# Turning the element-gradient tiles of a convolution stem through DRAM in one transfer, with reserves around transfers in the planned order

## The chip, the cores and the metric

The kernel runs on one core of one Trainium2 chip. The metric is device time in microseconds (us) of one execution. Three executions of the kernel before took 1305.70, 1307.24 and 1307.14 us; their median is 1307.14 us. A further execution was profiled, and its trace is what this document reads.

The engines are named as in the profile: PE (TensorE matmul), PEld (its weight load), DVE (VectorE), ACT (ScalarE), POOL (GpSimd) and SP (SyncE, which here only starts transfers). Transfers between DRAM and on-chip memory, and within on-chip memory, are DMAs; SP, ACT and POOL start them, each from its own queue and in program order.

## The reference

A strided convolution over time, a normalization over time for each batch and channel, and a GELU; and then all gradients of that for a given `grad_out`.

```python
B, T, D, K = 2, 16000, 256, 31          # x [2, 16000, 256], w [31, 256, 256], bf16
L = (T - K) // 2 + 1                    # 7985
h = sum(einsum('blc,cd->bld', x[:, i:i + 2 * L:2, :], w[i]) for i in range(K))
mu = h.sum(1)[:, None, :] / L
var = ((h - mu) ** 2).sum(1)[:, None, :] / L
h = (h - mu) / sqrt(var + 1e-5)
out = gelu(h * gn_gamma + gn_beta)      # tanh form
# returned: out, and the gradients of x, w, gn_gamma, gn_beta for grad_out
```

So there are three large products: the convolution itself, its transpose (the gradient of `x`, called the input gradient) and the correlation of `x` with the gradient at the convolution's output (the gradient of `w`).

## The kernel before

**Stages.** `forward` computes h for two batches b of four chunks c, from 0 to about 455 us. `input_grad` computes the gradient of x for the same eight chunks, from about 456 to 955 us. `weight_grad` ends the program. All three use a fast algorithm that adds and subtracts operands (on DVE) to need fewer products (on PE): each chunk goes through three branches A, B and C, and results in PSUM (four tiles `ps`) are moved, negated or combined by ACT (`keep`, L474; L917) and DVE (`ve`, `ve_neg`, L466 and L470) before PE can go on in the tile. A late ACT or DVE instruction there stops PE.

**The element-wise work in between.** `gelu_batch` and `gelu_unit` take h back from DRAM (`hd`, by a transfer from ACT's queue), take `grad_out` turned (a transposing transfer on SP, one for two units), compute out and the gradient before the normalization (ACT L714 to L738, DVE L718 to L740), store the latter (`dyd`, POOL) and turn out's tile for its store (a transposing transfer on SP). There are 16 units for each batch. Those of batch 0 run beside the forward pass of batch 1, and those of batch 1 beside the input gradient of batch 0.

`e_load` and `e_comp` make from `hd` and `dyd` the gradient at the convolution's output, for each chunk a tile `et` that has channels on partitions: two channel halves dh, two parities j and four phases k, with 256 positions each. It feeds PE at once. The weight gradient needs the same numbers with positions on partitions, and `dn_turn` makes them: 16 transposing transfers of 64 KB from `et` to the tile `DNO`, all on SP's queue, and then one POOL store of 1 MB to the DRAM tensor `dnd`. From `dnd`, `d2_piece` loads pieces (SP), takes differences (DVE, L1020) and stores them (`d2d`, POOL).

**What sets the order.** Every operation is first recorded by `Plan.add` with an engine, a duration and the tiles that it reads and writes. `Plan.order` then plays a schedule: each operation has a due time, worked out backwards from the position of the matmuls that need it (with `slack` for what no matmul needs soon; `PACE` gives the slack of the gelu units); at each step the engine that can start first takes its ready operation with the earliest due time. A transfer occupies its queue's engine for a while, then a shared server, and at most 8 may be under way for each of two groups. PE may take one of the next `look` matmul groups. The program is written in the order of the planned starts, and every engine then works through its own list in that order.

**Completion counters.** The built program has eight counters (DMAHW0 to DMAHW7) for the transfers that SP and ACT start, given out in turn, and eight more (DMASW0 to DMASW7) for POOL's. A transfer waits until the one that had its counter before has landed. Where such a wait stands in ACT's list, it holds all that follows on ACT.

Of the kernel before, what the change touches and what calls it, by code (L numbers as in the profile page):

```python
# [10 lines left out]
BF16 = mybir.dt.bfloat16  # L11
# [26 lines left out]
class Plan:  # L38
# [3 lines left out]
    def __init__(self, tc):  # L42
        self.tc = tc
        self.ops = []
        self.lastw = {}
        self.readers = {}
        self.pe = 0.0
        self.slack = 40.0
        self.hold = -1
        self.look = 6  # L50
        self.npe = 0

    def cells(self, ap):
# [48 lines left out]
    def order(self):  # L102
        ops = self.ops
# [5 lines left out]
        due = [0.0] * n  # L109
        for i in range(n - 1, -1, -1):  # L110
            o = ops[i]
# [8 lines left out]
        pes = [i for i, o in enumerate(ops) if o["eng"] == "PE"]  # L120
        rank = {i: k for k, i in enumerate(pes)}
        nextpe = 0
# [5 lines left out]
        free = {e: 0.0 for e in wait}  # L128
# [4 lines left out]
        while done < n:  # L133
# [27 lines left out]
                lane.append(end)  # L161
            ends[i] = end
            done += 1
            for s in succ[i]:
                r = end if ops[s]["eng"] == e and o["dma"] is None else end + 0.12
                if o["dma"] is not None and ops[s]["dma"] is not None:
                    r += 4.0
                ready[s] = max(ready[s], r)
                left[s] -= 1
                if not left[s]:  # L170
                    wait[ops[s]["eng"]].append(s)
# [15 lines left out]
def conv_stem_kernel(  # L187
# [28 lines left out]
    vl_d = [dram.tile([P, 3, 2, 2048], BF16, name=f"vl{i}") for i in range(3)]  # L216
    h_d = [[dram.tile([P, 4096], BF16, name=f"hd{b}_{c}") for c in range(NCK)] for b in range(NB)]
    dy_d = [[dram.tile([P, 4096], BF16, name=f"dyd{b}_{c}") for c in range(NCK)] for b in range(NB)]
    NDR = 192 + 8192 + 256
    dn_d = [dram.tile([NDR, D], BF16, name=f"dnd{b}") for b in range(NB)]  # L220
    d2_d = [dram.tile([9, P, 19 * D], BF16, name=f"d2d{b}") for b in range(NB)]
# [19 lines left out]
    def sb(off, *shape, dt=BF16):  # L241
        n = int(np.prod(shape)) * (2 if dt == FP32 else 1)
        assert off % 64 == 0 and off + 2 * n <= AR, (off, shape)
        v = arena[:, off // 2:off // 2 + n]
        if dt == FP32:
            v = v.bitcast(FP32)
        if len(shape) == 1:
            return v
        names = "abcdefg"[:len(shape)]
        return v.rearrange("p (" + " ".join(names) + ") -> p " + " ".join(names), **dict(zip(names, shape)))  # L250
# [5 lines left out]
    def load(out, in_, nbytes, run, eng="SP", slack=None, srcs=()):  # L256
        e = {"SP": nc.sync, "POOL": nc.gpsimd, "ACT": nc.scalar}[eng]
        add(eng, {"POOL": 0.8, "SP": 0.4, "ACT": 0.15}[eng], [out], [in_, *srcs], lambda: e.dma_start(out=out, in_=in_),  # L258
            dma=dcost(nbytes, run), slack=slack)

    def turn(out, in_, nbytes, slack=None):
        add("SP", 1.2 + max(0, nbytes - 262144) * 4.2e-6, [out], [in_],
            lambda: nc.sync.dma_start_transpose(out=out, in_=in_), dma=dcost(nbytes, 256), slack=slack)  # L263

    def zero(out, n, eng="POOL"):
# [565 lines left out]

    def dn_turn(b, c, o):
        et = ET[(4 * b + c) % 3]
        for dh in range(2):
            for j in range(2):
                for k in range(4):
                    turn(o[:, :, 4 * j + k, dh * P:(dh + 1) * P], et[:, dh, k, j, 0:HM], 65536)
        r0 = (192 if b else 0) + 2048 * c
        load(dn_d[b][r0:r0 + 2048, :].rearrange("(a p r) d -> p a (r d)", p=P, r=8),
             o.rearrange("p a r d -> p a (r d)"), 1 << 20, 4096, "POOL")  # L840

    def g_sums(t):
        et = ET[t % 3]
# [200 lines left out]
    DT = [sb(GREG, 15, D)]  # L1044
    D1T = sb(GREG + 7680, 2, 7, D)
    D2T = sb(GREG + 14848, 3, 2, 3, D)
    DNO = sb(GREG + 28928, 2, 8, D)


    xf = x.rearrange("b t c -> (b t) c")  # L1050
# [180 lines left out]

    RINGS = ((3, 2, 2, 2), (2, 1, 1, 2))
    D2AT = {(0, 0): (0, 1, 2), (0, 1): (3, 4), (1, 0): (5, 6)}
    PACE = ((15.0, 10.0), (40.0, 8.0))
    fw = forward()
    load_gb()
    add("DVE", 0.1, [JK], [], lambda: nc.vector.memset(JK, 0.0))
# [82 lines left out]
```

## Time and profile before

| | |
|---|---|
| median of three executions | 1307.14 us |
| profiled execution: its time, its span | 1306.86 us, 1305.1 us |
| PE busy, share of the span | 1235.0 us, 95% |
| DVE, ACT, POOL busy | 922.2, 492.5, 194.9 us |
| mean share of the 16 DMA engines, 450 to 850 us | 0.78 |
| transposing transfers on SP within on-chip memory | 160, of which 128 are those of `dn_turn` |

PE is busy nearly all the time, so time is to be found in the places where it stands still. A view that lists what each engine waited for, the timeline of one engine in a narrow window (idle time before an instruction stands in brackets with what ended it), and the chain of waits followed back from a late instruction show them. The view by windows gives the busy time of each engine in a stretch, then the clock that PE was granted (1.00 is full) and the mean busy share of the DMA engines.

### The profile page before, as it was taken

The page shows a single profiled execution, that of the slowest core. Times are in us where ns is not written, and L with a number is a line of the kernel's source. Part 1 is how long each engine was busy: PE and PEld are TensorE (multiplying, and loading weights), DVE is VectorE, ACT ScalarE, POOL GpSimd, SP SyncE. Part 2 cuts the span into 40 slices and gives each one's busy share as a digit, 9 for nine tenths or more (in the row PEclk, how much of TensorE's full clock was granted, in tenths as well). Part 3 has the DMA queues.
Part 4 walks back from the last instruction along what each step waited for, and adds up shares of the span by engine and source line. Part 5 has one row for each costly group of instructions (what it writes and reads, how often), then busy time and mean ns, then how long its engine had stood idle before and what let it go on. Part 6 is the DMA issues. An engine that isn't in the chain of part 4 may idle for free.

```text
span 1305.1 us, 19140 instructions
## 1 busy us (share of the span) xinstructions
PE 1235.0 (95%) x7746; PEld 759.7 (58%) x7746; DVE 922.2 (71%) x1164; ACT 492.5 (38%) x690; POOL 194.9 (15%) x293
## 2 busy tenths in 40 slices
PE   4999999999999989797899999899999999999998
PEld 2887799777778934343344444344466555556554
DVE  5978558789997678586786685557673885874462
ACT  0243243786863386566563223223221111112100
POOL 1002112111111011111120342123200000011021
PEclk9999999999999999898999999899999999999999
DMA  8644765959598869787784897768785698876610
GB/s 198 134 126 113 166 104 134 240 120 240 138 175 254 256 174 233 161 207 178 181 212 135 245 322 213 195 240 293 250 300 200 193 309 285 296 246 215 203 36 29
DMA packets 333177, 259.32 MB, mean 199 GB/s; under 512 B 195560, under 2 KB 311240, under 8 KB 326864
## 3 DMA queue, kind: packets, MB, share of 16 engines
q1 hardware_dynamic: 294448, 166.37, 51.4%
q0 software_dynamic: 21744, 83.34, 19.0%
q10 hardware_dynamic: 16896, 8.39, 2.6%
q8 instruction: 60, 0.98, 0.3%
q14 instruction: 29, 0.24, 0.1%
HBM read 128.32 MB, written 83.31 MB: 162 GB/s over the span
## 4 chain that ended last, share of the span: by engine, by line
PE 79%; DVE 7%; DMA 5%; SPq 3%; ACT 3%; issue 2%; POOL 0%; ACTq 0%; POOLq 0%; DVEq 0%
PE ps L391 32%; PE ps L1109 25%; PE ps L890 23%; SPq L263 2%; DVE arena L728 2%; DMA arena<-in_x_dram 1%; DMA arena<-in_grad_out_dram 1%; DMA arena<-dnd 1%; DMA arena<-arena 1%; DVE arena L849 1%; DVE ps L466 1%; DVE arena L718 1%; DMA d2d<-arena 1%; ACT arena L474 1%; DVE arena L1020 1%
## 5 line engine op out<-in xcount | busy, mean ns | idle before, releaser
L890 PE MATMUL ps<-arena 128*128 128x512 bf16 (+1 forms) x2112 | 459.9, 380 | 40.2 <-ACT ps L474 11.5
L391 PE MATMUL ps<-arena 128*128 128x256 bf16 (+3 forms) x3536 | 430.6, 283 | 19.4 <-DVE arena L349 17.7
L391 PEld LDWEIGHTS <-arena 128*128 128x128 bf16 x3536 | 345.9, 98 | 103.5 <-DVE arena L349 18.2
L890 PEld LDWEIGHTS <-arena 128*128 128x128 bf16 x2112 | 208.6, 99 | 291.0 <-issue 54.9
L1109 PE MATMUL ps<-arena 128*128 128x512 bf16 (+1 forms) x2016 | 343.8, 332 | 0.7 <-ACT ps L1202 0.7
L474 ACT ACTIVATE arena<-ps 128x1024 f32<-128x1024 f32 (+1 forms) x139 | 141.8, 1021 | 487.4 <-PE ps L890 219.6
L1109 PEld LDWEIGHTS <-arena 128*128 128x128 bf16 x2016 | 197.2, 98 | 144.1 <-issue 2.6
L359 DVE TENSOR_TENSOR arena<-arena 128x1088 bf16<-128x1088 bf16 (+3 forms) x182 | 155.4, 894 | 62.4 <-PE ps L391 54.5
L728 DVE TENSOR_TENSOR arena<-arena 128x1024 bf16<-128x1024 bf16 x160 | 109.6, 689 | 45.0 <-ACT arena L720 28.4
L258 POOL DMA_DIRECT2D out_dram<-arena x81 | 58.6, 726 | 457.3 <-DVE arena L1141 321.3
L1072 DVE TENSOR_TENSOR arena<-arena 128x4096 bf16<-128x4096 bf16 x42 | 95.4, 2287 | 34.3 <-DMA arena<-in_x_dram 25.6
L466 DVE TENSOR_TENSOR ps<-ps,arena 128x1024 f32<-128x1024 f32 x68 | 82.2, 1225 | 29.8 <-PE ps L1109 21.9
L849 DVE TENSOR_TENSOR arena<-arena 128x514 bf16<-128x514 bf16 (+3 forms) x152 | 71.4, 520 | 29.9 <-PE ps L890 28.7
L1020 DVE TENSOR_TENSOR arena<-arena 128x768 bf16<-128x768 bf16 (+3 forms) x112 | 63.7, 635 | 18.8 <-DMA arena<-dnd 18.3
L494 ACT ACTIVATE arena<-ps 128x512 bf16<-128x512 f32 (+1 forms) x64 | 37.1, 581 | 100.8 <-PE ps L391 99.4
L1190 DVE TENSOR_TENSOR arena<-arena 128x2304 bf16<-128x2304 bf16 x36 | 48.2, 1352 | 33.7 <-PE ps L1109 33.7
L258 POOL DMA_DIRECT2D d2d<-arena x70 | 50.8, 726 | 107.5 <-DVE arena L1020 100.2
L258 POOL DMA_DIRECT2D dyd<-arena x32 | 24.2, 758 | 229.3 <-DVE arena L728 208.6
L258 POOL DMA_DIRECT2D vl<-arena x36 | 26.1, 725 | 167.7 <-DVE arena L349 89.1
L474 ACT ACTIVATE ps<-ps 128x1024 f32<-128x1024 f32 x31 | 31.2, 1008 | 44.4 <-PE ps L1109 18.5
L718 DVE SCALAR_TENSOR_TENSOR arena<-arena 128x1024 bf16<-128x1024 bf16 x32 | 39.0, 1218 | 10.2 <-ACT arena L716 10.2
L349 DVE TENSOR_TENSOR arena<-arena 128x1024 bf16<-128x1024 bf16 (+2 forms) x37 | 36.8, 1016 | 7.6 <-DMA arena<-in_w_dram 5.2
(80 smaller groups left out, 638.7 us busy)
## 6 DMA issues: line engine op xcount, KB each, us to landing
arena<-in_x_dram SPq DMA_DIRECT2D x52, 1024.0 KB, 7.5
arena<-d2d SPq DMA_DIRECT2D x16, 1216.0 KB, 9.3
out_dram<-arena POOLq DMA_DIRECT2D x14, 1024.0 KB, 5.5
d2d<-arena POOLq DMA_DIRECT2D x30, 384.0 KB, 7.2
arena<-dnd SPq DMA_DIRECT2D x10, 960.0 KB, 7.0
vl<-arena POOLq DMA_DIRECT2D x36, 256.0 KB, 4.6
arena<-vl SPq DMA_DIRECT2D x9, 1024.0 KB, 5.8
hd<-arena POOLq DMA_DIRECT2D x8, 1024.0 KB, 6.0
```

Source lines behind the costliest of these rows:

```text
L258: add(eng, {"POOL": 0.8, "SP": 0.4, "ACT": 0.15}[eng], [out], [in_, *srcs], lambda: e.dma_start(out=out, in_=in_), dma=dcost(nbytes, run), ...
L359: lambda: nc.vector.tensor_tensor(out=o, in0=a, in1=b, op=ALU.add))
L391: yield nc.tensor.matmul(ps[:, dh, cs], lhsT=wt, rhs=mv, start=s0, stop=False, skip_group_check=True)
L466: add("DVE", dve(1024, 1), [out], [a, b], lambda: nc.vector.tensor_tensor(out=out, in0=a, in1=b, op=op))
L474: lambda: nc.scalar.activation(out=out, in_=ps, func=ACT.Copy, scale=scale))
L718: lambda: V.scalar_tensor_tensor(out=z, in0=y2, scalar=1.0 / GELU_A, in1=y, op0=ALU.add, op1=ALU.mult))
L728: add("DVE", dve(1024), [o], [a, b_], lambda: V.tensor_tensor(out=o, in0=a, in1=b_, op=op))
L849: lambda: nc.vector.tensor_tensor(out=o, in0=a, in1=b, op=ALU.add))
L890: yield nc.tensor.matmul(ps[:, e, 0:wide], lhsT=lt, rhs=mv, start=s0, stop=False, skip_group_check=True)
L1020: lambda: nc.vector.tensor_tensor(out=out, in0=a, in1=b_, op=ALU.subtract))
L1072: add("DVE", dve(4096), [o], [a, b], lambda: nc.vector.tensor_tensor(out=o, in0=a, in1=b, op=ALU.add))
L1109: yield nc.tensor.matmul(ps[:, s, c0:c1], lhsT=lt, rhs=mv, start=s0, stop=False, skip_group_check=True)
```

## The change

Three things are changed.

`dn_turn` no longer has 16 transposing transfers. Four POOL transfers of 256 KB write `et` to a new DRAM tensor `dnc` (256 channels by 2048 positions, one for each chunk), one transposing transfer of 1 MB on SP reads it back into `DNO`, which now has another order of its axes, and two POOL transfers of 512 KB store that to `dnd` in place of one of 1 MB.

The planner's picture of a transposing transfer is changed (the time that a large one holds SP), and so is its rule on transfers. Before, a transfer that follows a transfer is planned 4 us after the first one's end. Now there are three reserves (`pads`): up to 4 us before a transfer that follows other work, up to 4 us before one that follows a transfer, and up to 2 us before work, PE's left out, that follows a transfer; each at most 0.3 of the room that the due time leaves.

Four numbers are changed: the default slack (40 to 60), `look` (6 to 7), and `PACE`. The units of batch 1 were due 40 us after the matmul position at which they are recorded, plus 8 us for each unit; they are now due after 20 us plus 11 us for each.

```diff
-        self.slack = 40.0
+        self.slack = 60.0
         self.hold = -1
-        self.look = 6
+        self.look = 7
+        self.pads = (4.0, 4.0, 2.0)
...
+            slip = free["PE"] - due[pes[nextpe]] - ops[pes[nextpe]]["dur"] if nextpe < len(pes) else 0.0
             for s in succ[i]:
                 r = end if ops[s]["eng"] == e and o["dma"] is None else end + 0.12
-                if o["dma"] is not None and ops[s]["dma"] is not None:
-                    r += 4.0
+                room = max(0.0, due[s] + slip - r)
+                if ops[s]["dma"] is not None:
+                    r += min(self.pads[0 if o["dma"] is None else 1], 0.3 * room)
+                elif o["dma"] is not None and ops[s]["eng"] != "PE":
+                    r += min(self.pads[2], 0.3 * room)
...
+    dnc_d = [[dram.tile([D, 2048], BF16, name=f"dnc{b}_{c}") for c in range(NCK)] for b in range(NB)]
...
     def turn(out, in_, nbytes, slack=None):
-        add("SP", 1.2 + max(0, nbytes - 262144) * 4.2e-6, [out], [in_],
+        add("SP", 1.25 + max(0, nbytes - 262144) * 6e-6, [out], [in_],
...
     def dn_turn(b, c, o):
         et = ET[(4 * b + c) % 3]
+        m = dnc_d[b][c][:]
         for dh in range(2):
             for j in range(2):
-                for k in range(4):
-                    turn(o[:, :, 4 * j + k, dh * P:(dh + 1) * P], et[:, dh, k, j, 0:HM], 65536)
+                load(m[dh * P:(dh + 1) * P, 1024 * j:1024 * j + 1024].rearrange("p (k f) -> p k f", k=4), et[:, dh, :, j, 0:HM],
+                     262144, 512, "POOL")
+        turn(o.rearrange("p r a d -> p (r a) d"), m, 1 << 20)
         r0 = (192 if b else 0) + 2048 * c
-        load(dn_d[b][r0:r0 + 2048, :].rearrange("(a p r) d -> p a (r d)", p=P, r=8),
-             o.rearrange("p a r d -> p a (r d)"), 1 << 20, 4096, "POOL")
+        for a in range(2):
+            load(dn_d[b][r0 + 1024 * a:r0 + 1024 * a + 1024, :].rearrange("(p r) d -> p r d", r=8), o[:, :, a, :], 524288, 512, "POOL")
...
-    DNO = sb(GREG + 28928, 2, 8, D)
+    DNO = sb(GREG + 28928, 8, 2, D)
...
-    PACE = ((15.0, 10.0), (40.0, 8.0))
+    PACE = ((20.0, 13.0), (20.0, 11.0))
```

All lines after the new ones are shifted: L258 (`load`) becomes L264, L263 (`turn`) becomes L269, L474 becomes L480.

**SP's list at the second chunk of batch 0** (`dn_turn` of b = 0, c = 1). A row with `in_grad_out_dram` is a turned load of grad_out for two gelu units, `128x8x128` is the turning of out's tile, `128x2x128` is one of the 16 small transfers. Before:

```order
L263 DMA_TRANSPOSE arena<-arena 128x8x128
L263 DMA_TRANSPOSE arena<-in_grad_out_dram 128x8x256
L258 DMA arena<-hd_2_62 128x2x256
L263 DMA_TRANSPOSE arena<-arena 128x8x128
L258 DMA arena<-dyd_3_71 128x2x256
L263 DMA_TRANSPOSE arena<-arena 128x2x128 x16
L263 DMA_TRANSPOSE arena<-in_grad_out_dram 128x8x256
L263 DMA_TRANSPOSE arena<-arena 128x8x128 x2
```

Now:

```order
L269 DMA_TRANSPOSE arena<-arena 128x8x128
L269 DMA_TRANSPOSE arena<-dnc_1_77 128x16x256
L269 DMA_TRANSPOSE arena<-in_grad_out_dram 128x8x256
L264 DMA arena<-hd_2_62 128x2x256
L264 DMA arena<-dyd_3_71 128x2x256
L269 DMA_TRANSPOSE arena<-arena 128x8x128
```

One transfer stands where 16 stood, and the next turned load of grad_out stands right behind it instead of behind the 16.

**ACT's list at the same chunk**, with the counters that each instruction waits for. The row `arena<-hd_1_65` is the load of h for gelu unit 6 of batch 1; behind it stand the moves of PSUM tiles (L474 and L917, now L480 and L925) on which PE waits. Before:

```order
L714 ACTIVATE arena<-arena,stats 128x1024 [waits DMAHW5_49,DMAHW2_49]
L738 ACTIVATE arena,esum_95<-arena 128x1024 [waits DVE_49]
L716 ACTIVATE arena<-arena,stats 128x1024 [waits Activation_49]
L258 DMA arena<-hd_1_65 128x4x256 [waits DMAHW0_49,DVE_49]
L474 ACTIVATE ps_101<-ps_102 128x1024 [waits PE_49]
L917 ACTIVATE ps_104<-ps_104 128x512 [waits PE_49]
```

Now:

```order
L744 ACTIVATE arena,esum_103<-arena 128x1024 [waits DVE_49]
L722 ACTIVATE arena<-arena,stats 128x1024 [waits Activation_49]
L264 DMA arena<-hd_1_65 128x4x256 [waits DVE_49]
L480 ACTIVATE arena<-ps_110 128x1024 [waits PE_49]
L726 ACTIVATE arena<-arena 128x1024 [waits DMASW3_49,DVE_49]
```

Before, this load waited for a counter of SP's and ACT's transfers; now it waits for DVE alone.

**POOL's list at the same chunk.** `COPY` fills the edges of the next `et`, `dyd` and `out_dram` are stores of the gelu units and of results. Before:

```order
L258 DMA out_dram<-arena 128x4096
L258 DMA dyd_1_73<-arena 128x4x256
L258 DMA dnd_76<-arena 128x2x2048
L258 DMA dyd_1_73<-arena 128x4x256
L258 DMA out_dram<-arena 128x4x256 x2
```

Now:

```order
L830 COPY arena<-arena 128x2x2
L830 COPY arena<-arena 128x2
L264 DMA dnc_1_77<-arena 128x4x256 x4
L264 DMA out_dram<-arena 128x4096
L264 DMA dyd_0_72<-arena 128x4x256 x2
L264 DMA out_dram<-arena 128x4x256 x2
L264 DMA dnd_84<-arena 1024x1x256 x2
```

Four transfers to `dnc` are new, and two to `dnd` stand for one.

## The prediction

> **What bounds the kernel now.** I read the page first, then the busy time in three windows, then PE's timeline around each long stop, and last the chain of waits behind each stop.
>
> ```profile
> span 1305.1 us, 19140 instructions
> PE 1235.0 (95%) x7746; PEld 759.7 (58%) x7746; DVE 922.2 (71%) x1164; ACT 492.5 (38%) x690; POOL 194.9 (15%) x293
> ...
> 0.00:450.00 450.00, 426.52 (x3537) 346.04 (x3538) 358.87 (x476) 214.93 (x367) 64.19 (x99) 1.00 0.75 171
> 450.00:850.00 400.00, 360.55 (x1673) 165.41 (x1671) 277.04 (x429) 199.30 (x233) 79.69 (x122) 0.96 0.78 205
> 850.00:1305.10 455.10, 447.92 (x2541) 248.28 (x2538) 286.30 (x259) 78.30 (x90) 51.01 (x72) 1.00 0.67 220
> ...
> PE ps L391 <- DVE arena L349: 17.7, 2, 14.8
> ```
>
> PE is the bound: it stands still for 1305.1 - 1235.0 = 70.1 us, of which 17.7 is the start (first loads), which the change does not touch. The middle window holds 400 - 360.55 = 39.5 us of it, and it alone has a granted clock under 1.00. That is the stretch in which `dn_turn` runs. PE's timeline shows four stops there, and the windows right after them (columns: PE, PEld, DVE, ACT, POOL, clock, DMA share, GB/s) show that PE then works on at half clock:
>
> ```profile
> 531.56 1.01 PE L890 MATMUL ps<-arena 128*128 128x512 bf16 x2 [10.64 <-ACT ps L474]
> 613.56 1.86 PE L890 MATMUL ps<-arena 128*128 128x512 bf16 x4 [7.92 <-DVE ps L466]
> 650.12 1.44 PE L890 MATMUL ps<-arena 128*128 128x512 bf16 x3 [6.28 <-ACT ps L917]
> 823.77 1.44 PE L890 MATMUL ps<-arena 128*128 128x256 bf16 x4 [5.44 <-DVE ps L470]
> ...
> 531.60:535.10 3.50, 3.50 (x9) 1.24 (x9) 1.69 (x3) 3.47 (x5) 0.00 (x0) 0.51 0.44 105
> 613.60:617.00 3.40, 3.40 (x9) 1.17 (x9) 3.37 (x6) 2.91 (x3) 0.00 (x0) 0.51 0.29 77
> 650.20:654.60 4.40, 4.40 (x11) 1.50 (x11) 1.57 (x2) 3.93 (x4) 0.00 (x0) 0.51 0.49 113
> 823.80:828.60 4.80, 4.80 (x14) 2.00 (x14) 3.00 (x6) 0.00 (x0) 0.00 (x0) 0.50 1.08 160
> ```
>
> So a stop costs its idle time and about half of the slow stretch behind it: 10.64 + 1.7 = 12.3 us, 7.92 + 1.7 = 9.6, 6.28 + 2.2 = 8.5 and 5.44 + 2.4 = 7.8. Together 38.2 us. The other 9.2 us of the window's idle time are many gaps of 0.3 to 1.7 us.
>
> What ends each stop is in SP's and ACT's timelines and in the chain of waits:
>
> ```profile
> 516.35 22.54 SPq L263 DMA_TRANSPOSE arena<-arena  x16
> ...
> 527.67 2.34 DMA arena<-arena
> 530.09 0.37 ACTq L258
> 530.50 1.02 ACT ps L474
> ...
> 573.54 20.85 SPq L263 DMA_TRANSPOSE arena<-arena  x16
> 596.65 8.31 SPq L263 DMA_TRANSPOSE arena<-in_grad_out_dram  x1
> ...
> 596.65 13.67 DMA arena<-in_grad_out_dram
> ...
> 610.41 0.69 DVE L728 TENSOR_TENSOR arena<-arena 128x1024 bf16<-128x1024 bf16 x1 [9.57 <-DMA arena<-in_grad_out_dram]
> ...
> 646.66 2.34 DMA arena<-arena
> 649.07 0.37 ACTq L258
> ...
> 812.63 9.10 DMA d2d<-arena
> 822.58 1.15 DVE ps L470
> ```
>
> First and third stop: ACT's list holds a load of h (ACTq L258) that waits for a completion counter, and the counter's last user is the ninth of the 16 small transfers of a chunk; ACT stands until that has landed (527.67 + 2.34 = 530.01), and PE waits for the PSUM move behind it (L474, L917). Second stop: 16 transfers hold SP for 20.85 us; the turned load of grad_out stands behind them, starts at 596.65 and lands 13.7 us later, when DVE has waited 9.57 us for it in L728; `ve` (L466) stands behind that, and PE behind `ve`. Fourth stop: DVE waits for stores of d2 pieces that take 9.10 us to land. It has no small transfer in it.
>
> **The change, part by part.** It removes 128 small transfers, adds 8 large ones on SP and 40 on POOL, moves loads ahead of their users, and spreads the gelu units. The prices:
>
> ```profile
> L263 SPq DMA_TRANSPOSE arena<-arena x144: 1168/1245/5690, 466.6 to 841.6; - x144
> L263 SPq DMA_TRANSPOSE arena<-in_grad_out_dram x7: 1500/3805/8314, 482.0 to 658.4; - x7
> ...
> L263 SPq DMA_TRANSPOSE arena<-in_x_dram x2: 13307/13560/13812, 303.3 to 363.4; - x2
> ...
> L258 POOL DMA_DIRECT2D dnd<-arena x8: 705/707/719, 497.2 to 846.1; - x8
> ...
> dyd<-arena POOLq DMA_DIRECT2D x16, 256.0 KB, 4.0
> ```
>
> *SP.* A chunk held SP for 16 x 1.245 = 19.9 us at least (20.85 and 22.54 above). A turn from DRAM of 0.5 MB (grad_out) held it for 1.5 to 8.3 us, median 3.8; two of x, of 2.2 and 2.0 MB (272 and 240 rows of 8 KB), for 13.3 and 13.8. A 1 MB transfer lies between: 3.8 to 13.8. I take 7, since 0.5 MB gives twice 3.8 and 2.1 MB half of 13.6. It also waits for its four stores, of which one such as `dyd` takes 4.0 us to land; as long as POOL starts them early enough, that is over by then. SP gains some 13 us in every chunk.
>
> *ACT's counters.* In the changed list no load of h has a `dn_turn` transfer as the last user of its counter (unit 6: DVE alone). So the cause of the first and third stop is gone, not just shortened: 12.3 + 8.5 = 20.8 us. The second stop had SP late by one burst; with 13 us less in front, the load that came 9.57 us late comes in time: 9.6 us. The sum of the three is 30.4. Where the stop goes: ACT and DVE are then next, with 199.3 and 277.0 busy us of 400 in that window; 370 us suffice for both.
>
> *Fourth stop.* It hangs on the DMA engines, which the change does not relieve; but the reserve of up to 2 us before DVE work behind a transfer puts the subtractions later in DVE's list, behind `ve_neg`. Bounds 0 and 7.8; I take half, 3.9.
>
> *POOL* gets 5 more transfers in each chunk, 40 x 0.71 = 28 us on an engine that is busy for 79.7 of 400: off the path. If it were not, the edge copies and `dyd` stores behind the two `dnd` stores would be late.
>
> *DMA engines.* These are the same 16 for all queues. Their time in three windows (packets, MB, share):
>
> ```profile
> q1 hardware_dynamic: 1722, 0.39, 25.4%
> ...
> q1 hardware_dynamic: 5145, 1.32, 87.8%
> q10 hardware_dynamic: 519, 0.26, 20.6%
> ...
> q0 software_dynamic: 9623, 39.38, 29.8%
> ...
> 482.00:521.00 39.00, 35.70 (x166) 16.14 (x165) 33.94 (x53) 26.50 (x31) 9.19 (x13) 1.00 1.00 238
> ```
>
> The first (522.5 to 530) holds small transfers alone: 0.254 x 7.5 / 0.39 = 4.9 us of all 16 engines for 1 MB. The second (366 to 376) has a turn from DRAM: 0.878 x 10 / 1.32 = 6.7. POOL's stores (third, 450 to 850) cost 0.298 x 400 / 39.38 = 3.0, and the 512-byte load of h on q10 0.206 x 10 / 0.26 = 7.9. A chunk now adds a write of 1.05 MB (3.2 at POOL's rate, 8.3 at q10's) and 1.9 for the turn; the two smaller `dnd` stores add 0 to 5.1. That is 5.1 to 15.3 us for each chunk, 41 to 122 for eight. The stage's share is 0.78 x 400 = 312 us, but it is uneven: 1.00 from 482 to 521. What lands there comes later. The lower bound is nearest, as the new stores are POOL's; of its 5.1 us in each of the four chunks beside gelu I charge a quarter, 5 us in all (bounds 0 and 20).
>
> *Elsewhere.* Slack, `look` and `PACE` reorder the other stages too, but their gaps are small: 70.1 - 39.5 - 17.7 = 12.9 us with the tail. I take 0, between -5 and +5.
>
> Sum: 1306.9 - 30.4 - 3.9 + 5 = 1277.6, so 1278 us. The profiled execution is 0.3 us under the median of the runs, which is nothing here.
>
> **Rivals.**
>
> *One stop stays.* The 1 MB transfer waits at the head of SP's queue for its four stores, and the turned load of grad_out stands right behind it. With 13.6 us on SP and one store as late as 7 us it holds the queue as long as the burst did. For it: the window with share 1.00. Against it: the reserves put loads earlier. It costs the second stop again, and the fourth whole: 1277.6 + 9.6 + 3.9 = 1291.
>
> *Slower: the DMA engines become the stage's bound.* The place is the window 450 to 850, the price the detour through DRAM. It decides from (400 - 312) / 8 = 11 us more for a chunk on; at 12 us it gives 1315, at the upper bound of 15.3 the stage needs 312 + 122 = 434 us instead of 400, so 1341. For it: 1.00 and 1.08 in the windows above. Against it: the rate that POOL's stores show over 39 MB.
>
> *No change.* The waits are only passed on: SP is held as long by other transfers, and each counter has some late user. Then 1307. The Trainium skill, "DMA: Bandwidth & Descriptors", section "Issuing engines are not separate DMA queues", has a rule that points here: where a DMA is started saves only the time to initiate it, "which is usually small relative to the DMA itself"; by that rule, fewer starts for the same bytes are worth nothing and the time stays at 1307. This trace differs: in the burst, starting took 1.245 us for each small transfer while the engines were 25.4% busy.
>
> **How the numbers follow.** The forecast, 1263 (fourth stop wholly gone, no contention, small gaps shorter) to 1284, has 0.57. One stop stays, to 1303: 0.25. DMA-bound, slower: 0.11. No change: 0.07. A measurement can tell 0.2% (2.6 us) from nothing. Faster is 0.57 + 0.25 = 0.82, same 0.07, slower 0.11. The range 1263 to 1303 leaves out the last two cases.
>
> **What would show it.** Right: small transfers on SP fall from 160 to 32; eight of `dnc` hold SP for 4 to 14 us; ACT L474 and L917 no longer wait for `arena<-arena`; PE is busy for over 97% of the stage and the half-clock stretches fall from four to one or none. Wrong: DVE L728 still waits some 10 us for grad_out (one stop stays), or the DMA share of the stage is above 0.95 with PE waiting behind DVE and ACT for `hd`, `dyd` or `d2d` (slower); or new stops of 5 us and more stand in the stages that I took as untouched.

## The result

The changed kernel takes 1272.4 us (median of four executions, 1267.4 to 1278.1) against 1307.2 (1305.7 to 1308.0): a ratio of 0.973, with an interval of 0.970 to 0.976. The profiled execution took 1271.8 us, so it may stand for the rest. 1278 was predicted, 1263 to 1303 as the range.

The page of the changed kernel (span, busy times, then packets, MB and share of the 16 DMA engines for the two large queues):

```profile
span 1270.0 us, 19007 instructions
PE 1225.3 (96%) x7676; PEld 758.6 (60%) x7746; DVE 923.3 (73%) x1164; ACT 491.1 (39%) x690; POOL 230.4 (18%) x333
...
q1 hardware_dynamic: 290608, 166.35, 53.0%
q0 software_dynamic: 24432, 91.73, 22.2%
```

The view by windows for the middle of the program, and for the one stretch that still has a low clock (PE, PEld, DVE, ACT, POOL, clock, DMA share, GB/s); then PE's timeline at the longest stop that is left in this stage:

```profile
450.00:850.00 400.00, 388.21 (x1797) 179.98 (x1832) 307.49 (x480) 210.88 (x246) 123.59 (x174) 0.99 0.94 255
528.40:535.20 6.80, 5.85 (x16) 2.31 (x16) 6.55 (x9) 0.82 (x2) 4.00 (x8) 0.50 1.06 367
```

```profile
529.35 77.77 PE L898 MATMUL ps<-arena 128*128 128x256 bf16 x345 [3.07 <-DVE ps L476]
```

PE is busy for 388.2 of 400 us where it was for 360.6, and its longest stop there is 3.07 us where there were four of 5.4 to 10.6. At the same time the DMA engines are busier: 0.94 instead of 0.78. The whole difference lies in the input gradient. From its first matmul to the first of the weight gradient it took 500 us and takes 463 (the forward pass 454.5 and 453.0, the weight gradient to the end 350.7 and 354.0). The view by windows of exactly this stage, before and after:

```profile
454.50:954.50 500.00, 459.82 (x2116) 208.75 (x2115) 349.19 (x529) 227.32 (x262) 106.72 (x160) 0.97 0.78 216
```

```profile
453.00:916.00 463.00, 450.87 (x2070) 207.41 (x2112) 354.93 (x542) 227.84 (x262) 139.12 (x196) 0.99 0.91 252
```

Of the 37 us, 28 are idle time (40.2 to 12.1) and 9 are busy time that became shorter. In place of four half-clock stretches there is one: 16.1 us before, 6.8 now, so (16.1 - 6.8) / 2 = 4.7 us of the 9; some 40 matmul records of this stage are missing in the second trace, so part of the rest is only not seen.

How long the turns of `dnc` hold SP (count, then least, median and longest time in ns), and the longest rows of what DVE and ACT wait for in the stage (us in total, times, longest):

```profile
L269 SPq DMA_TRANSPOSE arena<-dnc x8: 4123/7280/12784, 464.3 to 786.2; - x8
```

```profile
DVE arena L734 <- DMA arena<-in_grad_out_dram: 10.1, 4, 4.7
ACT arena L480 <- DMA out_dram<-arena: 8.1, 3, 4.5
```

And the time from issue to landing (last column, median us) of two kinds of transfers in the stage. Before:

```profile
dyd<-arena POOLq DMA_DIRECT2D x16, 256.0 KB, 4.0
...
arena<-hd ACTq DMA_DIRECT2D x14, 256.0 KB, 4.2
```

After:

```profile
dyd<-arena POOLq DMA_DIRECT2D x16, 256.0 KB, 9.9
...
arena<-hd ACTq DMA_DIRECT2D x14, 256.0 KB, 8.1
```

This is the reading that the experiments have to explain. Both take longer than before, a load of h 8.1 us in place of 4.2, and yet ACT and DVE together wait less for transfers: summed over all their rows of the view of waits between 450 and 960 us it is 23.9 us, where it was 56.4.

### The profile page after: what moved, and what is told of

Its sections match the earlier page's. It is cut to its first block, busy times and chain, and to the rows that moved or that the text cites. A ratio compares the mean times of both kernels' runs of the same rounds, so it can differ in the third digit from the quotient of the medians.

```text
span 1270.0 us, 19007 instructions
## 1 busy us (share of the span) xinstructions
PE 1225.3 (96%) x7676; PEld 758.6 (60%) x7746; DVE 923.3 (73%) x1164; ACT 491.1 (39%) x690; POOL 230.4 (18%) x333
## 4 chain that ended last, share of the span: by engine, by line
PE 80%; DMA 8%; DVE 7%; issue 2%; ACT 2%; SPq 1%; POOL 0%; POOLq 0%; ACTq 0%; DVEq 0%
PE ps L397 29%; PE ps L1117 26%; PE ps L898 25%; DMA arena<-in_grad_out_dram 5%; DMA arena<-hd 2%; DVE arena L734 2%; DVE arena L724 1%; ACT arena L480 1%; DVE arena L820 1%; SPq L269 1%; DVE arena L815 0%; DMA arena<-in_w_dram 0%; SPq L264 0%; DVE arena L746 0%; DVE arena L1080 0%
## 5 line engine op out<-in xcount | busy, mean ns | idle before, releaser
L898 PE MATMUL ps<-arena 128*128 128x512 bf16 (+1 forms) x2069 | 451.0, 377 | 12.2 <-ACT ps L480 3.7
L1117 PE MATMUL ps<-arena 128*128 128x512 bf16 (+1 forms) x1989 | 342.5, 331 | 3.9 <-DVE ps L472 2.5
L480 ACT ACTIVATE arena<-ps 128x1024 f32<-128x1024 f32 (+1 forms) x139 | 141.8, 1022 | 472.6 <-PE ps L898 188.1
L365 DVE TENSOR_TENSOR arena<-arena 128x1087 bf16<-128x1087 bf16 (+3 forms) x182 | 153.8, 893 | 58.7 <-PE ps L397 51.0
L264 POOL DMA_DIRECT2D out_dram<-arena x81 | 58.2, 721 | 446.8 <-DVE arena L1149 316.7
L472 DVE TENSOR_TENSOR ps<-ps,arena 128x1024 f32<-128x1024 f32 x68 | 82.3, 1226 | 37.6 <-PE ps L1117 26.4
L857 DVE TENSOR_TENSOR arena<-arena 128x516 bf16<-128x516 bf16 (+3 forms) x152 | 71.6, 521 | 34.4 <-PE ps L898 34.2
L264 POOL DMA_DIRECT2D d2d<-arena x70 | 50.7, 726 | 92.0 <-DVE arena L1028 85.3
L264 POOL DMA_DIRECT2D dyd<-arena x32 | 24.2, 757 | 171.4 <-DVE arena L734 165.8
L264 POOL DMA_DIRECT2D vl<-arena x36 | 26.0, 724 | 154.6 <-DVE arena L355 90.7
L724 DVE SCALAR_TENSOR_TENSOR arena<-arena 128x1024 bf16<-128x1024 bf16 x32 | 39.0, 1220 | 12.3 <-ACT arena L722 12.0
L480 ACT ACTIVATE ps<-ps 128x1024 f32<-128x1024 f32 x31 | 31.2, 1008 | 37.0 <-PE ps L1117 21.7
L476 DVE SCALAR_TENSOR_TENSOR ps<-ps,arena 128x1024 f32<-128x1024 f32 x24 | 29.5, 1229 | 21.4 <-ACT arena L480 9.5
```

The source lines that it names most:

```text
L365: lambda: nc.vector.tensor_tensor(out=o, in0=a, in1=b, op=ALU.add))
L472: add("DVE", dve(1024, 1), [out], [a, b], lambda: nc.vector.tensor_tensor(out=out, in0=a, in1=b, op=op))
L480: lambda: nc.scalar.activation(out=out, in_=ps, func=ACT.Copy, scale=scale))
L724: lambda: V.scalar_tensor_tensor(out=z, in0=y2, scalar=1.0 / GELU_A, in1=y, op0=ALU.add, op1=ALU.mult))
L857: lambda: nc.vector.tensor_tensor(out=o, in0=a, in1=b, op=ALU.add))
L898: yield nc.tensor.matmul(ps[:, e, 0:wide], lhsT=lt, rhs=mv, start=s0, stop=False, skip_group_check=True)
```

## The experiments

The change has two halves, the transfers ("detour") and the planned order (reserves, slack, `look`, `PACE`). The first two kernels do one half alone; the third and the fourth take one suspect away. Ratios are against runs of the kernel before on the same chip, with their interval; "stage" is the time from the first matmul of the input gradient to the first of the weight gradient, from each trace.

### 1. The detour alone

The kernel before with these parts of the change, and none of its planner:

```diff
-        add("SP", 1.2 + max(0, nbytes - 262144) * 4.2e-6, [out], [in_],
+        add("SP", 1.25 + max(0, nbytes - 262144) * 6e-6, [out], [in_],
...
-                for k in range(4):
-                    turn(o[:, :, 4 * j + k, dh * P:(dh + 1) * P], et[:, dh, k, j, 0:HM], 65536)
+                load(m[dh * P:(dh + 1) * P, 1024 * j:1024 * j + 1024].rearrange("p (k f) -> p k f", k=4), et[:, dh, :, j, 0:HM],
+                     262144, 512, "POOL")
+        turn(o.rearrange("p r a d -> p (r a) d"), m, 1 << 20)
```

> The kernel before with the new transfers alone (four stores to a DRAM scratch, one 1 MB turn, two dnd stores); the planner's reserves, slack, look and PACE are the old ones. Theory A, the 16 small transfers made the stops (they hold SP for 20 us and stand ahead of ACT's loads of h in the completion counters): first three stops gone, the fourth stays, so 1306.9 - 30.4 + 5 = 1281 us (1274 to 1288); ACT no longer waits for arena<-arena. Theory B, the reserves in the planner and the new PACE bring the gain: 1300 to 1307. Theory C, the detour itself is dear (DMA engines) and the reserves pay for it: over 1307.

Measured: 1323.7 us, ratio 1.012 (1.007 to 1.017). Slower, so A is wrong as a statement on the transfers alone. The stage is 489.0 us, 11 less than before and 26 more than in the changed kernel; and PE stands still at the entry of the weight gradient. PE's timeline there, and SP's:

```profile
958.99 1.01 PE L1112 MATMUL ps<-arena 128*128 128x256 bf16 x4 [13.59 <-issue]
968.76 1.03 PE L1112 MATMUL ps<-arena 128*128 128x256 bf16 x4 [8.76 <-DMA arena<-d2d]
```

```profile
944.96 0.47 SPq L259 DMA_DIRECT2D arena<-d2d  x1
...
957.31 1.82 SPq L259 DMA_DIRECT2D arena<-d2d  x1
```

The first loads of the weight gradient start when PE already needs them. In the stage itself no stop is over 5.2 us, but ACT and DVE wait 80.5 us in all for transfers, now mostly for loads of `hd`. Rows of the view of waits:

```profile
DVE arena L810 <- DMA arena<-hd: 22.8, 2, 12.3
ACT arena L715 <- DMA arena<-hd: 20.6, 4, 10.9
```

### 2. The order alone

The changed kernel with the old `dn_turn`, `DNO` and `dnd` store:

```diff
-        turn(o.rearrange("p r a d -> p (r a) d"), m, 1 << 20)
+                for k in range(4):
+                    turn(o[:, :, 4 * j + k, dh * P:(dh + 1) * P], et[:, dh, k, j, 0:HM], 65536)
```

> The changed kernel with the old 16 small transfers and the old dnd store; the planner's reserves, slack 60, look 7 and the new PACE stay. Theory A: the loads of h now stand earlier, so more of them (seven by the planned order, before four) stand behind a small transfer in their counter; ACT waits over 20 us for arena<-arena and the time is 1300 to 1320 us, no gain. Theory B: 1272 to 1282 us, nearly the whole gain.

Measured: 1347.8 us, ratio 1.029 (1.026 to 1.032); the stage is 532 us, and PE stands still for 12.72 us just before it. B is out, and A was too mild. ACT waits for small transfers more than before, 27.1 us in `keep` alone. Two rows of the view of waits:

```profile
DVE arena L1025 <- DMA arena<-dnd: 29.4, 6, 8.7
ACT arena L479 <- DMA arena<-arena: 27.1, 3, 10.4
```

So each half alone, planned for itself, makes the kernel slower, and both together make it 2.7% faster.

### 3. The shared counter taken away

The kernel before; the loads of h are the only transfers that ACT starts.

```diff
-        e = {"SP": nc.sync, "POOL": nc.gpsimd, "ACT": nc.scalar}[eng]
+        e = {"SP": nc.sync, "POOL": nc.gpsimd, "ACT": nc.gpsimd}[eng]
```

> The kernel before; only the 16 loads of h of the gelu units are started by POOL in place of ACT, from the same places of the planned order. POOL's transfers count on other counters than SP's. Theory A: the first and the third stop of PE (behind ACT L474 and L917) are gone or under 2 us, the second and the fourth stay: 1307 - 12.3 - 8.5 = 1286 us (1282 to 1297). Rival, the loads of h only showed a lateness that the DMA engines cause: the waits move to the loads themselves and the time stays at 1302 to 1310.

Measured: 1301.4 us, ratio 0.994 (0.992 to 0.996): 7 us, a third of what A says. The prediction put the first and the third stop down to the counter. With the counter free, both are gone from the matmuls before which they stood. But two others stand 128 and 105 matmuls later, with another cause, and the second stop, before the same matmul as ever, has grown from 7.92 to 10.00 us. PE's timeline at the three, and DVE's and SP's around the first:

```profile
553.16 2.29 PE L890 MATMUL ps<-arena 128*128 128x512 bf16 x5 [6.16 <-ACT arena L474]
...
609.39 3.10 PE L890 MATMUL ps<-arena 128*128 128x512 bf16 x7 [10.00 <-DVE ps L466]
...
666.16 1.15 PE L890 MATMUL ps<-arena 128*128 128x512 bf16 x4 [4.28 <-ACT arena L474]
```

```profile
545.62 0.69 DVE L728 TENSOR_TENSOR arena<-arena 128x1024 bf16<-128x1024 bf16 x1 [7.43 <-DMA arena<-in_grad_out_dram]
```

```profile
519.91 20.36 SPq L263 DMA_TRANSPOSE arena<-arena  x14
540.37 2.21 SPq L263 DMA_TRANSPOSE arena<-in_grad_out_dram  x1
```

The burst holds SP for 20 us, the turned load of grad_out stands behind it, DVE waits for that, ACT for DVE, PE for ACT (before the third, DVE waits 7.85 us for the same). The counter was the first of two latenesses that one burst makes. Of the 16.9 us of idle time that went with it, the second brought back 6.16 + 4.28 + 2.08 = 12.5.

### 4. The old numbers with the new rule

The changed kernel:

```diff
-        self.slack = 60.0
+        self.slack = 40.0
-        self.look = 7
+        self.look = 6
-    PACE = ((20.0, 13.0), (20.0, 11.0))
+    PACE = ((15.0, 10.0), (40.0, 8.0))
```

> The changed kernel with slack 40, look 6 and the old PACE; the detour and the new rule of reserves stay. Theory A: the numbers only move gaps of 1 to 2 us: within 6 us of the changed kernel, 1268 to 1280. Theory B (spreading the gelu units is needed for the detour): 1285 and more, with stops of PE of over 4 us in 450 to 850.

Measured: 1297.6 us, ratio 0.991 (0.989 to 0.993). Neither theory had the place. The stage is 457 us, shorter even than in the changed kernel, and ACT and DVE wait 12.3 us in it for transfers; but the forward pass ends at 485.8 us and not at 453, with stops (10.01, 5.38 and 3.39 us) in the half where the gelu units of batch 0 run beside it. The longest:

```profile
350.43 1.86 PE L397 MATMUL ps<-arena 128*128 128x256 bf16 x8 [10.01 <-DMA arena<-in_x_dram]
```

With the new rule the numbers are worth 32 us in the forward pass (485.8 against 453.0; with the old rule and the old numbers it ended at 454.5), and nothing in the stage that the change is about. There it is the rule of the reserves that counts.

### 5. Why the detour alone comes late at the end

The planner of `detour_only` (with `slip` as in the change):

```diff
-                    r += 4.0
+                    r += min(4.0, 0.3 * max(0.0, due[s] + slip - r))
```

> As detour_only, but the planner's fixed 4 us between one transfer and the next that needs it become min(4, 0.3 x room), so nothing where the chain is late already. Theory D, detour_only lost its 22 us at the entry of the weight stage because the last chunk's chain (stores, turn, dnd stores, seven pieces of d2, first load of the weight stage) is one step longer and pays 4 us at each step: that stop (13.6 + 8.8 us) falls under 4 us, the gradient stage stays near 489 us, and the time is 1302 us (1295 to 1308). Rival, the first loads of the weight stage are late because the DMA engines are loaded: the stop stays, 1318 to 1325.

Measured: 1313.1 us (1302 to 1322 in ten executions), ratio 1.003 (0.999 to 1.006); the profiled one took 1307.0. PE goes from the input gradient to the weight gradient without a stop, so the 22 us were the fixed 4 us at every step of a chain that was late already, as theory D says; and the stage is 490.8 us, as it says. The time is only half as much better as D says, since a new stop of 12.35 us stands at 787 (below, under what was not expected).

### 6. and 7. The same orders, the other transfers

Experiments 1 and 2 also move instructions. The next two do not: the planner sees the same operations, and only what is issued in the place of the transposing ones differs.

In `dn_turn` of the kernel before, where each of the 16 is issued (`same_order_detour`):

```diff
+            if seen.count((dh, j)) == 4:
+                yield nc.gpsimd.dma_start(out=m[...], in_=et[:, dh, :, j, 0:HM])
+            if len(seen) == 16:
+                yield nc.sync.dma_start_transpose(out=on.rearrange("p r a d -> p (r a) d"), in_=m)
```

In that of the changed kernel, where the turn is issued (`same_order_small`):

```diff
+            for dh in range(2):
+                for j in range(2):
+                    for k in range(4):
+                        yield nc.sync.dma_start_transpose(out=o[:, 4 * j + k, :, dh * P:(dh + 1) * P], in_=et[:, dh, k, j, 0:HM])
```

> The kernel before with its planned order kept to the instruction; only where a chunk's 16 small transfers stood, four stores and one turn are issued (each store in the place of its fourth small transfer, the turn in the place of the sixteenth), and two dnd stores in the place of one. Theory A (small transfers hold SP and couple the counters): the first three stops go, 1307 - 30.4 + 5 = 1282 us (1275 to 1292). Rival E, the traffic of the detour makes every load land later and this order has its loads only 5 to 8 us ahead: the stops are replaced by waits for h, hd, dyd, 1298 to 1315.

> The changed kernel with its planned order kept to the instruction; only the four stores to the scratch are left out and 16 small transfers are issued in the place of the one turn. Theory A: stops of 5 to 10 us come back, ACT or DVE wait over 15 us in all behind SP's bursts, 1290 to 1315 us. Rival F, the order with its reserves carries the gain and the kind of transfer does not matter: 1266 to 1278 us, with the DMA share of 450 to 850 back under 0.85.

Measured, as a table of ratios to the kernel before (stage in us, and the time that ACT and DVE wait for transfers in it):

| | 16 small transfers | detour |
|---|---|---|
| order of before | 1 (500; 56.4) | 0.994, 0.991 to 0.997 (491.9; 62.1) |
| order of the change | 1.014, 1.008 to 1.019 (521.2; 82.3) | 0.973, 0.970 to 0.976 (463.1; 23.9) |

In the old order the detour is worth 0.6%, some 8 us (E has the time right, A has not). In the new one it is worth 4%, some 53 us (A is right, and too mild). Or read by columns: the new order costs 18 us with the small transfers and brings 28 with the detour. What ACT and DVE wait for in the stage, from the view of waits, first with the detour in the old order, then with the small transfers in the new one:

```profile
DVE arena L1037 <- DMA arena<-dnd: 23.9, 5, 12.2
DVE arena L729 <- DMA arena<-in_grad_out_dram: 11.8, 2, 8.1
DVE arena L810 <- DMA arena<-hd: 8.8, 1, 8.8
```

```profile
ACT arena L480 <- DMA arena<-arena: 20.3, 2, 12.0
ACT arena L480 <- DMA out_dram<-arena: 17.8, 3, 12.2
ACT ps L931 <- DMA arena<-arena: 8.1, 1, 8.1
```

In the first, E names the loads of h, `hd` and `dyd`; the longest waits are for `dnd` and grad_out, and `hd` comes third. Here PE goes through the same matmuls in the same order as in the kernel before, so the stops can be compared one by one. The first and the third are gone, and of the fourth 0.97 us is left (5.44 before). The second stays, with 6.44 us (7.92 before). Two are new, of 7.09 and 10.79 us, and one of 1.49 has grown to 4.48. One set of stops is exchanged for another of nearly the same length.

The second stop is a rival of the prediction come true: one stop stays. The turn waited at the head of SP's queue until 584.86 for the last of its four stores (started at 580.38, landed at 584.71), and the turned load of grad_out behind it started only 4.5 us sooner than in the kernel before. SP's timeline, DVE's and PE's:

```profile
584.86 4.19 SPq L845 DMA_TRANSPOSE arena<-dnc  x1
...
592.17 9.78 SPq L264 DMA_TRANSPOSE arena<-in_grad_out_dram  x1
```

```profile
606.35 0.69 DVE L729 TENSOR_TENSOR arena<-arena 128x1024 bf16<-128x1024 bf16 x1 [8.06 <-DMA arena<-in_grad_out_dram]
```

```profile
609.51 1.87 PE L907 MATMUL ps<-arena 128*128 128x512 bf16 x4 [6.44 <-DVE ps L467]
```

The longest of the new stops is of the same kind. A 1 MB turn holds SP for 17 us, the load of `dnd` starts 19 us after the turn did, DVE waits for it for 12.2 us, and PE behind DVE. SP's timeline and PE's:

```profile
739.35 17.42 SPq L845 DMA_TRANSPOSE arena<-dnc  x1
...
758.17 0.47 SPq L259 DMA_DIRECT2D arena<-dnd  x1
```

```profile
775.00 1.44 PE L907 MATMUL ps<-arena 128*128 128x512 bf16 x3 [10.79 <-DVE ps L467]
```

### 8. More traffic

Where the changed kernel issues a store to `dnc`:

```diff
+            for mm in (m, dnx_d[b][c][:]):
+                yield nc.gpsimd.dma_start(out=mm[...], in_=et[:, dh, :, j, 0:HM])
```

> The changed kernel, same planned order, but each of the 32 stores to the scratch is issued twice, the second time to a scratch that nobody reads: 8.4 MB more, about 25 to 35 us of all 16 engines, and 24 us of POOL. Theory G, the reserves absorb it: 1272 + 0 to 8 us, DMA share of 450 to 850 near 0.98. Rival, the DMA engines are the stage's bound now: 1272 + 20 to 30, so 1292 to 1302 us.

Measured: 1289.1 us, ratio 0.985 (0.978 to 0.992), so some 15 us more than the changed kernel. The busy time of the engines grew by 27 us over the whole run (79.6% of 1289.4 against 78.7% of 1270.0, all queues). The answer lies between the two, nearer to the rival:

```profile
450.00:850.00 400.00, 372.91 (x1712) 169.33 (x1710) 293.02 (x454) 201.68 (x236) 141.06 (x191) 0.98 0.97 256
```

PE's longest stop is 4.2 us; ACT and DVE wait 66.6 us for transfers. POOL, which had the extra stores to start, is at 141 of 400 us, so the engines and not POOL are the likelier cause, but these two were not told apart.

### 9. The counter again, in the new order

`same_order_small` with the edit of the third experiment:

```diff
+        e = {"SP": nc.sync, "POOL": nc.gpsimd, "ACT": nc.gpsimd}[eng]
```

> same_order_small with the 16 loads of h of the gelu units started by POOL from their places in the order, so that they count on other counters than SP's transfers. There ACT waited 34 us in all for arena<-arena. If the shared counters are the larger part of what small transfers cost in this order: those waits fall under 8 us and the time from 1328 to 1295 to 1308 us. If SP being held for 20 us is the larger part: 1315 us and more, with DVE or ACT waiting for the turned grad_out or for hd and dyd in their place.

Measured: 1342.1 us, ratio 1.026 (1.022 to 1.029): slower still. ACT's waits in L480 and in the other move of a PSUM tile (L931) for small transfers are gone; these stand in their place:

```profile
DVE arena L734 <- DMA arena<-in_grad_out_dram: 29.6, 5, 14.3
ACT arena L720 <- DMA arena<-arena: 26.5, 3, 11.2
```

So freeing the counter does not bring the time back. But the edit moves the loads of h into a list that waits for the burst too: POOL's store to `dnd` needs all 16 small transfers, and four times POOL stood still before it for 14 to 17 us, with a load of h behind it. POOL's timeline at one of them:

```profile
586.91 1.73 POOL L264 DMA_DIRECT2D dnd<-arena  x2 [14.99 <-DMA arena<-arena]
...
589.23 0.91 POOL L264 DMA_DIRECT2D arena<-hd  x1
```

What the counters alone cost in this order therefore stays open; that the burst holds the list in which a load stands is what both places share.

### 10. and 11. Which reserve

The changed kernel, first `no_reserve_ahead`, then `no_reserve_behind`:

```diff
-        self.pads = (4.0, 4.0, 2.0)
+        self.pads = (0.0, 4.0, 2.0)
```

```diff
-        self.pads = (4.0, 4.0, 2.0)
+        self.pads = (4.0, 4.0, 0.0)
```

> The changed kernel with pads (0, 4, 2): no reserve ahead of a transfer that waits for an engine's result. If this reserve is what lets the order live with the detour: the gradient stage grows from 463 to 480 us and more (detour_room, without it, has 491), 1290 to 1305 us. If it is the reserve behind a transfer: under 1282 us (the planned end is 6 us later than the changed kernel's).

> The changed kernel with pads (4, 4, 0): no reserve between a transfer and the work of ACT, DVE or POOL that needs it. Its planned order has a stop of 7.5 us at the entry of the gradient stage. If this reserve carries the gain: 1295 us and more, with ACT and DVE waiting over 20 us more for landings (h, hd, grad_out, dnd) than in the changed kernel. If the one ahead of transfers does: 1272 + 11 = 1283 us, 1276 to 1290.

Measured: 1287.1 us, ratio 0.985 (0.980 to 0.989), stage 473.8, waits 46.6; and 1293.0, 0.989 (0.986 to 0.992), stage 480.3, waits 48.0, with the planned stop at the entry (8.32 us) beside it. Both lie between the theories. Each reserve is worth 11 to 17 us of the stage, and without either one the waits for transfers double. By the rule they act from two sides: the one has a transfer stand later in its queue than its data are due, so that a late result blocks the queue less, the other has the user stand later behind the transfer. How much of the 53 us either would bring alone stays open, as each edit also moves the rest of the order.

What the two bring together can be read from two kernels above. `detour_room` and `after_old_numbers` have the detour and the old numbers, and differ only in the reserves: (0, 4, 0) in the first, (4, 4, 2) in the second. The stage goes from 490.8 to 457.0 us and the waits of ACT and DVE for transfers in it from 67.7 to 12.3. The forward pass is longer with them at these numbers: it ends at 461.7 and at 485.8.

### 12. Other numbers

```diff
-        self.slack = 60.0
+        self.slack = 70.0
-        self.look = 7
-        self.pads = (4.0, 4.0, 2.0)
+        self.look = 8
+        self.pads = (6.0, 4.0, 2.0)
...
-    PACE = ((20.0, 13.0), (20.0, 11.0))
+    PACE = ((15.0, 13.0), (20.0, 10.0))
```

> The changed kernel with other numbers only: pads (6, 4, 2), slack 70, look 8, PACE ((15, 13), (20, 10)), whose planned order ends 4.2 us sooner. If the planned end carries over to the chip as it did for the changed kernel (planned 1271.4, span 1270.0): 1268 us, 1262 to 1274. If the engines of DMA, at 0.94 in the middle stage, decide and not the plan: 1272 to 1285.

Measured: 1278.0 us (six executions), ratio 0.977 (0.974 to 0.980): not better than the changed kernel. Its stage is 468.7 us, and a stop of 6.41 us stands in the forward pass. A planned end 4 us earlier is not worth 4 us on the chip.

## Why the prediction was right, and where its steps were not

**The sum.** 1277.6 against 1271.8 in the profile. The sign, the place (the input gradient) and the signs named came out: eight turns of `dnc` hold SP for 4.1 to 12.8 us with a median of 7.28 (7 was taken), no PSUM move waits for a small transfer, PE is busy for 97.05% of 450 to 850, one half-clock stretch is left, the DMA share is 0.94. The four stops had 30.3 us of idle time, and one of 3.07 is left; with the 4.7 of the half-clock stretches that is 31.9 us, where 30.4 + 3.9 = 34.3 had been credited. The small gaps closed by 0.8 us, and 4.3 us of shorter busy time are not explained (some of it are missing records). That makes the 37 us of the stage; 1.5 came in the forward pass, and 3.3 were lost at the end. The charge of 5 us for contention cannot be read off. That the time is only 5.8 us from the forecast is luck in part, since several terms were wrong and made up for each other.

**The step that failed** is the one from the transfers to the stops: "The cause of the first and third stop is gone, not just shortened: 12.3 + 8.5 = 20.8", and for the second "with 13 us less in front, the load that came 9.57 us late comes in time". As a statement on what the whole change does it holds; as a statement on the transfers it does not. With the old order they bring 8 us of the 30.4: the load of the second stop starts 4.5 us sooner and not 13, and new stops stand where there were none. Three parts were misjudged:

- *Contention.* It was put at 5 us beside an unchanged order. Its size in engine time was right. The two large queues have 51.4% and 19.0% on the page of before, the others 3.0%, so 73.4% of 1305.1 us; after, with 3.5% for the others, it is 78.7% of 1270.0. That is 41.6 us more, 5.2 for each chunk, the lower bound (5.1). But it does not act as a charge of a quarter. It makes loads and stores land later (h 8.1 for 4.2, `dyd` 9.9 for 4.0), and an order that has them just in time then waits for them: 62.1 us in the old order with the detour, 80.5 in `detour_only`.
- *The order.* The reserves got half of the fourth stop and nothing else. The order as a whole (reserves and numbers) carries the rest: 28 us with the detour in place. With the small transfers it costs 18.
- *The fourth stop.* "It has no small transfer in it" misreads the trace of before. DVE's waits for stores of d2 pieces there are 0.16 and 0.30 us. Its long wait came earlier, before L812, the first work on a newly loaded `dyd`; the view finds no releaser for it, but it ends as that load lands. The load started at 802.04, right behind a burst, and took 3.0 us. In the 17 us from there to `ve_neg` (L470, at 822.50) DVE was idle for 2.9. DVE's timeline and SP's:

```profile
805.15 1.43 DVE L812 TENSOR_SCALAR arena<-arena,stats 128x2064 bf16<-128x2064 bf16 x2 [7.73 <-issue]
```

```profile
778.33 22.98 SPq L263 DMA_TRANSPOSE arena<-arena  x15
...
802.04 0.55 SPq L258 DMA_DIRECT2D arena<-dyd  x1
```

So a burst stands behind all four stops. It fits that with the transfers alone exchanged 0.97 us of the fourth is left, though PE had lost 10.79 us there some 42 us earlier; with the counter alone freed it keeps 5.42. The half that was credited to a reserve of 2 us was the transfers' work, and the other half, which was not credited, came as well.

**ACT's counters.** The mechanism was in the trace of before, and its row (10.64 us behind L474) was read rightly. But when a second lateness from the same burst follows, most of the stop comes back a few matmuls later; `before_h_by_pool` brings 7 us of 20.8, and `small_h_by_pool` none.

**The rivals.** One stop stays: this is what the detour in the old order shows, at the second stop (6.44 us) and again in a new place (10.79). In the changed kernel it is there in a mild form: before the one stop that is left, DVE waits 3.03 us for a turned load of grad_out that SP started right behind a turn of `dnc` (506.01, 7.56 us). Slower, DMA-bound: not reached, though the point from which it decides (11 us more for a chunk) was too far. The extra stores add 27 / 8 = 3.4 us to the 5.2, so 8.6 in all, and already cost 15 us (POOL's time for starting them included). No change: the rule of the Trainium skill, "DMA: Bandwidth & Descriptors", section "Issuing engines are not separate DMA queues", says that starting DMAs from several engines saves only the time that it takes to start them, which is usually small beside the DMA itself. By it, fewer starts would be worth nothing; in the new order the small transfers cost 53 us against the detour, which moves more bytes. The measurement decides: where 16 starts hold a queue for 20 us with other loads behind them, starting is the cost.

**Elsewhere** was taken as 0 and is 0 in sum: the forward pass is 1.5 us shorter, the end 3 us longer. But it is 0 only because the numbers were changed along with the rule; with the old ones the forward pass loses 32 us (experiment 4).

## What to carry to other kernels

Here a transfer that was made cheaper for its queue and dearer for the DMA engines paid well only in an order that has its loads further ahead, and that order paid only once no burst stood in their queue. Two such halves are to be costed together, as each alone can lose. When a stop hangs on one late transfer, look for the second latest behind the same cause before the whole stop is credited. The last wait before a stop need not be the long one: look back along the engine that ended it. A fixed reserve of 4 us was paid at every step of a chain that was late already (22 us in `detour_only`); one that shrinks with the room that is left was not.

## What the runs showed that was not expected

A 1 MB turn from DRAM has no fixed price. SP is held by it for 3.9 us at the least and 28.8 at the most (both in `detour_room`), though the same eight transfers are issued. There, the turn and the 1 MB and 384 KB stores of POOL run at the same time; SP's timeline, the windows and the DMA queues (packets, MB, share of the 16 engines; then KB each and us to landing) at that place (pieces of `d2d` took 17.6 us to land, median of five):

```profile
770.58 28.81 SPq L265 DMA_TRANSPOSE arena<-dnc  x1
```

```profile
770.00:786.00 16.00, 16.00 (x78) 7.45 (x76) 9.86 (x17) 4.05 (x5) 5.06 (x8) 1.00 1.09 195
786.00:799.00 13.00, 0.89 (x5) 0.29 (x3) 2.17 (x3) 0.84 (x1) 0.71 (x1) 0.74 1.21 134
```

```profile
q1 hardware_dynamic: 3173, 1.76, 71.6%
...
arena<-dnc SPq DMA_TRANSPOSE x1, 36.2
```

The engines are taken as fully busy (1.09 and 1.21), but they move 195 and 134 GB/s, where the changed kernel's stage has 252 at a share of 0.91. In 30 us, q1 took 0.716 x 30 = 21.5 us of all engines for 1.76 MB, so 12.2 us for each MB, where a turned MB had cost 6.7; and the 1.76 MB hold a load of `dnd` of 0.98 MB, so the turn alone may have cost more. The Trainium skill, "DMA: Bandwidth & Descriptors", section "Latency and other measured facts", gives 261 GB/s as the effective rate of a transposing DMA; by an estimate from that page a MB would take 3.8 us. Neither row agrees, and the measurement decides.

The 1 MB store of results that is under way there lands late, ACT's next `keep` needs its buffer, and PE stops. ACT's timeline and PE's:

```profile
798.16 1.02 ACT L476 ACTIVATE arena<-ps 128x1024 bf16<-128x1024 f32 x1 [15.34 <-DMA out_dram<-arena]
```

```profile
799.24 2.29 PE L894 MATMUL ps<-arena 128*128 128x512 bf16 x5 [12.35 <-ACT arena L476]
```

`no_reserve_behind` shows the same picture (27.1 us on SP, a stop of 12.22). That turns and stores slow each other is what these rows suggest; it was not tried by itself, and which of the two gives way stays open.
